# Product 3 of a unit placed behind product 1 of the next, and weight conversions held behind the gates, in a three-layer float32 kernel

## The chip, the cores and the metric

The kernel runs on one core of one Trainium2 chip. The metric is device time in microseconds (us). Engines are named as in the profile: PE is TensorE (PEld its weight loads), DVE is VectorE, ACT is ScalarE, POOL is GpSimd, and SP issues DMAs.

## The reference

Three layers in a row, all in float32:

```python
xread = softmax(x @ state.T / 8) @ state          # attention both ways, 8 batches x 8 heads
sread = softmax(state @ x.T / 8) @ x
x = concat(xread, sread)                          # 8 x 544 = 4352 tokens x 512
h = maximum(x[mask_e] @ w1[e], 0); x[mask_e] = h @ w2[e]     # 8 experts, 544 tokens each
g, val = x @ w_gate, x @ w_val                    # 512 -> 1536
out = (silu(g) * val) @ w_out                     # 1536 -> 512
```

The change touches only the third layer's first half, the gated products `x @ w_gate` and `x @ w_val`.

## The kernel before

**Stages.** Attention and routing run up to about 222 us, the experts' products up to 630 us, the gated passes from 630 to 1160 us, and the output products from 1160 to the end. Every float32 product is made of three matmuls on values split into a high and a low part.

**The gated passes.** A unit computes gate and value of 512 tokens for 256 of the 1536 hidden columns. There are two passes (`p`), each over nine groups of tokens (`groups`, lines 1159 and 1161: the experts 0 to 7, and the group E of the 256 tokens left over), each group with three units (`jj`), so 54 units. They are called unit 0 to unit 53 here; the code's `V = 27 * p + 3 * n + jj` (line 1249) is that number. The group E is the fifth of a pass, units 12 to 14 and 39 to 41.

A full unit (`unit`, from line 1116) multiplies blocks in the Winograd form of Strassen's method: seven block products in the order `PORDER = (1, 6, 7, 5, 2, 4, 3)` (line 868). Each product is a `hid`, 12 matmuls of 128x128 by 256 columns, so a full unit has 84; a unit of group E has four (48 matmuls). The passes have 4320 matmuls, all on line 1106.

The results go through four PSUM banks, each with two buffers, used by every second unit. Bank 1 takes product 1 and then, added to it, product 2; bank 2 takes product 6 and, after that has been read, product 4; bank 3 takes product 7; bank 4 takes product 5 and then, added to it, product 3. Behind the products stand, in this order: ACT's copy s1 of product 1 (line 1136), and on DVE u2 = product 6 + s1 (1139), u3 = product 7 + u2 (1142), `cs[:, :, 2]` = bank 4 + u3 (1145, the read of product 5), the gate of bank 1 (1148), `cs[:, :, 1]` = u3 - product 4 (1151), `cs[:, :, 0]` = bank 4 + u2 (1154, with product 3), and the gate of the three parts of cs (1155). A gate (`gate`, line 1112) is a silu on ACT (1113) and a multiplication on DVE (1114), 256 wide for bank 1 and 768 wide for cs. The unit's result m is then stored by SP (1157). s1, u2, u3 and cs have one buffer each, m has two.

**What runs beside it.** `after` (line 1226) splits the sums for the next group's operands into high and low parts between the products: one cast on ACT (871) and one subtraction on DVE (872) each. POOL makes the sums (897 to 900, 909 to 912), which SP stores (885) and loads again (890) in the second pass. SP also loads the inputs of the sums (926, 962, 1195).

The third layer's weights arrive as 64-bit numbers. `convert` (line 174) turns a block of 512 KB into float32: one instruction on ACT (179), three on DVE (181, 182, 184) and a store by SP (185); `load64` (line 162) loads a block (171). The first 16 conversions run beside the experts, the last 20 in the gated passes: conversion 16 + i is written behind the unit `CT[i]`, that is behind units 2, 4, ..., 22 and 30, 32, ..., 46, and the load of the next block behind it, the first ones behind units 0 and 28 (lines 1250 to 1255). The raw buffer is single in this stage.

**What sets the order.** The order in which instructions are written is a priority only. A planner goes through them with its own estimate of times and lists, for each engine, what is ready first, so that work can stand earlier in an engine's queue than it is written. Each engine, and SP's DMA queue, then runs its list in order. `tc.issue_after(ins)` holds the instructions written inside it behind `ins` in the list of `ins`'s engine. `hooks` is the kernel's dictionary of such instructions.

Of the kernel before, what the change touches and what calls it, by code (L numbers as in the profile page):

```python
# [26 lines left out]
AF = mybir.ActivationFunctionType  # L27
OP = mybir.AluOpType
# [3 lines left out]
B, H, S, D, NS = 8, 8, 512, 64, 32  # L32
# [25 lines left out]
def moe_kernel(ctx: ExitStack, tc: tile.TileContext, x, state, moe_w_gate, moe_w1, moe_w2,  # L58
               moe2_w_gate, moe2_w_val, moe2_w_out, out):
    nc = tc.nc  # L60
# [34 lines left out]
    xcs, hooks = {}, {}  # L95
# [1013 lines left out]
    def hid(p, a, b, start, stop):  # L1109
        product(p, [(lambda x, q, k=k: a[:, x, q, k], lambda y, k=k: b[:, y, k]) for k in range(2)], start, stop)  # L1110

    def gate(m, g, v):
        nc.scalar.activation(m, g, AF.Silu)  # L1113
        nc.vector.tensor_tensor(m, v, m, OP.mult)

    def unit(key, j, gi, after):
        m = cw.tile([128, 4, 256], F32, name="m", bufs=2)
        if gi == E:
            b1, b2 = bank(1), bank(2)
            hid(b1, WC[j, 1], Y[key, 1], True, False)  # L1120
            hid(b1, WC[j, 2], Y[key, 2], False, True)
            gate(m[:, 0], b1[:, 0], b1[:, 1])
            after(1)
            hid(b2, WC[j, 5], Y[key, 1], True, False)
            hid(b2, WC[j, 4], Y[key, 4], False, True)
            gate(m[:, 1], b2[:, 0], b2[:, 1])
            after(2)
            nc.sync.dma_start(m_d[gi][:, j], m[:, :2])
            return
        b1, b2, b3, b4 = (bank(i) for i in range(1, 5))  # L1130
        A = {n: WC[j, n] for n in PORDER}
        B = {n: Y[key, n] for n in PORDER}
        s1, u2, u3 = half("s1"), half("u2"), half("u3")
        cs = cw.tile([128, 2, 3, 256], F32, name="cs")
        hid(b1, A[1], B[1], True, False)
        nc.scalar.copy(s1, b1)
        after(1)
        hid(b2, A[6], B[6], True, True)
        nc.vector.tensor_tensor(u2, b2, s1, OP.add)
        after(6)  # L1140
        hid(b3, A[7], B[7], True, True)
        nc.vector.tensor_tensor(u3, b3, u2, OP.add)
        after(7)
        hid(b4, A[5], B[5], True, False)
        nc.vector.tensor_tensor(cs[:, :, 2], b4, u3, OP.add)  # L1145
        after(5)
        hid(b1, A[2], B[2], False, True)
        gate(m[:, 0], b1[:, 0], b1[:, 1])
        after(2)
        hid(b2, A[4], B[4], True, True)  # L1150
        nc.vector.tensor_tensor(cs[:, :, 1], u3, b2, OP.subtract)
        after(4)
        hid(b4, A[3], B[3], False, True)
        nc.vector.tensor_tensor(cs[:, :, 0], b4, u2, OP.add)  # L1154
        gate(m[:, 1:], cs[:, 0], cs[:, 1])
        after(3)
        nc.sync.dma_start(m_d[gi][:, j], m)

    groups = [[0, 1, 2, 3, E, 4, 5, 6, 7], [7, 6, 5, 4, E, 3, 2, 1, 0]]
    CT = tuple(range(2, 24, 2)) + tuple(range(30, 48, 2))  # L1160
# [60 lines left out]
    for p, n, gi, jj in hidden_units:  # L1221
        nxt = groups[p][n + 1] if n < E else None
        if jj == (p == n == 0) and nxt is not None:
            ysrc = y_sums(nxt, y_load(nxt, cw), cw)

        def after(step):
            if nxt is None or (gi == E) != (step < 3 and gi == E):
                return
            if gi == E:
                todo = {(0, 1): (0, 1), (0, 2): (1, 2), (1, 1): (2, 3), (1, 2): (3, 4), (2, 1): (4, 5), (2, 2): (5, 7)}  # L1230
                a, b = todo[jj, step]
                todo = PORDER[a:b]
            else:
                todo = {(1, 1): (1,), (1, 7): (6,), (1, 5): (7,), (2, 1): (5,), (2, 6): (2,), (2, 2): (4,),
                        (2, 5): (3,)}.get((jj, step), ())
            for m in todo:
                if m in ysrc:
                    y_combo((p, nxt), m, ysrc)

        if n == E and p == 0 and jj == 0:  # L1240
            wraw = pair_load(3, cw)
        unit(key, 3 * p + jj, gi, after)
        a = {1: 0, 3: 1, 4: 2, 6: 3}.get(n) if p else None
        if a is not None:
            if jj == 1:
                early = acts_load(*outs[a])
            elif jj == 2:
                acts_sums(outs[a][0], early, f"a{a}")
        V = 27 * p + 3 * n + jj
        if V in CT:  # L1250
            convert(16 + CT.index(V), cw)
        if V in CT or V in (0, 28):
            c = sum(t <= V for t in CT)
            if c < len(CT) and V != 22:
                load64(16 + c, cw, nc.sync)
        k = {2: 0, 5: 1, 7: 2}.get(n) if p else {1: 0, 3: 1, 6: 2}.get(n)
        if k is not None and jj == 1:
            early2 = out_load(k) if p else pair_load(3 + k, cw)
        if k is not None and jj == 2:
            if p:  # L1260
                out_sums(k, early2)
            else:
                pair_sums(early2, cw, f"w{3 + k}")
        if n == E and p == 0:
            src = pair_sums(wraw, cw, f"w{3 + jj}")
            if jj < 2:
                wraw = pair_load(4 + jj, cw)
            for m in PORDER:
                pair_combo(3 + jj, m, src)
        if n == E and p == 1:  # L1270
            src = out_sums(jj, out_load(jj))
            for m in PORDER:
                out_combo(jj, m, src)
            if jj == 1:
                acts[0] = acts_sums(outs[0][0], acts_load(*outs[0]), "a0")
                acts_prep(0, slice(0, 7))
        if jj == 2 and nxt is not None:
            key = (p, nxt)
        elif jj == 2 and p == 0:
            key = (0, gi)  # L1280
# [15 lines left out]
    def out_product(p, gi, jj, n, w, start, stop):  # L1296
        a, b = AO[gi, jj, n], WO[jj, w]
        product(p, [(lambda x, q, r=r: a[:, x, r, 128 * q:128 * q + 128], lambda y, r=r: b[:, y, r])
                    for r in range(2)], start, stop)

    BANK = {1: 1, 6: 2, 7: 3, 5: 4, 2: 1, 4: 2, 3: 3}
    for s, (gi, jj) in enumerate(outs):
        first, last = jj == 0, jj == 2
        if s + 1 < len(outs):
            acts[s + 1] = acts_sums(outs[s + 1][0], acts_load(*outs[s + 1]), f"a{s + 1}" if s + 1 < EARLY else None)
        if gi == E:
            if first:
                bx, by = bank(1), bank(2)
                o = rows()
            out_product(bx, gi, jj, 1, 1, first, False)  # L1310
            acts_prep(s + 1, slice(0, 3))
            out_product(bx, gi, jj, 2, 2, False, last)
            acts_prep(s + 1, slice(3, 5))
            if last:
                nc.scalar.copy(o[:, :, :256], bx)
            out_product(by, gi, jj, 3, 3, first, False)
            acts_prep(s + 1, slice(5, 7))
            out_product(by, gi, jj, 7, 7, False, last)
            if last:
                nc.vector.tensor_copy(o[:, :, 256:], by)  # L1320
                for q in range(2):
                    scatter(gi, q, o[:, q])
            continue
        if first:
            P = {n: bank(BANK[n]) for n in PORDER}
            s1, u2, u3 = half("s1"), half("u2"), half("u3")
            w = cw.tile([128, 2, 3, 256], F32, name="cs")[:, :, 0]
            oa, ob = rows(), rows()
        for m, n in enumerate(PORDER):
            out_product(P[n], gi, jj, n, n, first, last)  # L1330
            acts_prep(s + 1, slice(m, m + 1))
            if not last:
                continue
            if n == 1:
                nc.scalar.copy(s1, P[1])
            elif n == 6:
                nc.vector.tensor_tensor(u2, P[6], s1, OP.add)
            elif n == 7:
                nc.vector.tensor_tensor(u3, P[7], u2, OP.add)
            elif n == 2:  # L1340
                nc.vector.tensor_tensor(oa[:, :, :256], P[2], s1, OP.add)
            elif n == 5:
                nc.vector.tensor_tensor(ob[:, :, 256:], P[5], u3, OP.add)
                nc.vector.tensor_tensor(w, P[5], u2, OP.add)
            elif n == 4:
                nc.vector.tensor_tensor(ob[:, :, :256], u3, P[4], OP.subtract)
                for q in range(2):
                    scatter(gi, 2 + q, ob[:, q])
            else:
                nc.vector.tensor_tensor(oa[:, :, 256:], P[3], w, OP.add)  # L1350
                for q in range(2):
                    scatter(gi, q, oa[:, q])
# [29 lines left out]
```

## Time and profile before

| | us |
|---|---|
| median of 3 runs | 1431.58 (1429.67 to 1432.13) |
| the profiled execution's own time | 1430.67 |
| its span, first to last instruction | 1428.6 |
| mean granted clock of PE | 0.979 |

The span is the time between the first and the last instruction that the profile has; the execution's own time is what the median is made of. Engines run side by side, so busy times don't add up, and an engine's idle time counts only where the end of the kernel hangs on it. In a timeline, equal instructions that follow each other are merged into one row, and the brackets at a row's end tell how long the engine was idle before it and which instruction's end it waited for. The granted clock is the share of TensorE's full clock that it was given: 1.00 is 2.4 GHz, and the other level is 1.2 GHz, so a mean between the two tells how the time was divided.

### The profile page before, as it was taken

Reading aid. Unit: us, or ns where it says so; the run is one execution under the profiler, and the core shown is the slowest. Engines: PE = TensorE matmul, PEld = TensorE weight load, DVE = VectorE, ACT = ScalarE, POOL = GpSimd, SP = SyncE. Lnnn points to the kernel's source line nnn. Section 1 sums busy time; section 2 is a strip of 40 time slices with the busy share of each in tenths; the row PEclk is TensorE's granted clock in tenths of the full one; section 3 lists DMA queues with packets and bytes.
Section 4 is the critical chain, followed back from the end, with each engine's and each line's share of the span. In section 5 each row is a group of like instructions: output and inputs, shape, how many; then the busy total and the mean of one; then the engine's idle time right before and its main releaser. Section 6 shows DMA issues by size and latency. Waiting matters only on the chain.

```text
span 1428.6 us, 28982 instructions
## 1 busy us (share of the span) xinstructions
PE 1358.8 (95%) x11448; PEld 1318.8 (92%) x11449; DVE 1065.7 (75%) x2067; ACT 571.6 (40%) x1124; POOL 445.3 (31%) x388
## 2 busy tenths in 40 slices
PE   6998489999999999999989999999999999999997
PEld 5876288999999999999989999999999999999996
DVE  5889778877987664649776766777666588998982
ACT  5885123333433343434333333433333364444440
POOL 5776201010201010425241300112211008778862
PEclk9999699999999999999999999999999999999998
DMA  7542325543554464356674644756766394344431
GB/s 134 130 117 94 114 69 192 197 147 117 169 169 135 143 217 129 128 178 230 233 254 150 218 166 146 264 181 248 248 250 219 114 313 137 132 145 151 149 104 45
DMA packets 123335, 238.36 MB, mean 167 GB/s; under 512 B 47808, under 2 KB 57024, under 8 KB 116800
## 3 DMA queue, kind: packets, MB, share of 16 engines
q1 hardware_dynamic: 110096, 209.75, 44.0%
q0 software_dynamic: 5536, 17.83, 3.7%
q10 hardware_dynamic: 7568, 8.95, 2.1%
q8 instruction: 89, 1.46, 0.4%
q14 instruction: 46, 0.38, 0.1%
HBM read 153.65 MB, written 82.84 MB: 166 GB/s over the span
## 4 chain that ended last, share of the span: by engine, by line
PE 79%; DVE 8%; issue 5%; DMA 3%; ACT 3%; POOL 1%; SPq 0%; ACTq 0%; POOLq 0%; DVEq 0%
PE b L1106 48%; PE h L828 13%; PE y L847 4%; PE y L843 4%; PE y L844 4%; PE bt L807 1%; DVE yb L872 1%; DMA raw<-in_moe_w_val_dram 1%; DMA raw<-y_d 1%; PE pt L236 1%; PE ps L363 1%; PE acc L483 1%; ACT xu L325 1%; DMA xg<-xm_d,idx 0%; ACT RBh L220 0%
## 5 line engine op out<-in xcount | busy, mean ns | idle before, releaser
L1106 PE MATMUL b<-yb,w 128*128 128x256 f32 x4320 | 519.7, 283 | 10.0 <-DVE cs L1145 8.1
L1106 PEld LDWEIGHTS b<-yb,w 128*128 128x128 f32 x4320 | 517.2, 191 | 12.5 <-DVE cs L1145 9.2
L1106 PE MATMUL b<-w,yb 128*128 128x256 f32 x2160 | 257.5, 282 | 0.0
L1106 PEld LDWEIGHTS b<-w,yb 128*128 128x128 f32 x2160 | 257.4, 189 | 0.0
L828 PE MATMUL h<-xh,w 128*128 128x288 f32 (+1 forms) x1024 | 210.7, 298 | 1.5 <-issue 0.9
L828 PEld LDWEIGHTS h<-xh,w 128*128 128x128 f32 x1024 | 163.7, 191 | 3.2 <-DVE hl L833 1.1
L872 DVE TENSOR_TENSOR yb<-tt,yb 128x512 fp32r<-128x512 f32 x164 | 145.3, 897 | 16.8 <-ACT yb L871 14.3
L798 POOL DMA_INDIRECT xg<-xm_d,idx x38 | 44.2, 1163 | 361.3 <-PE bt L807 158.6
L897 POOL TENSOR_TENSOR tt<-raw 128x512 f32<-128x512 f32 (+1 forms) x33 | 42.8, 1299 | 340.8 <-DMA raw<-m_d 141.1
L828 PE MATMUL h<-xl,w 128*128 128x288 f32 (+1 forms) x512 | 148.2, 292 | 0.7 <-DVE xl L813 0.7
L872 DVE TENSOR_TENSOR yb<-raw,yb 128x512 fp32r<-128x512 f32 x127 | 131.6, 1043 | 15.9 <-ACT yb L871 12.0
L871 ACT CAST yb<-tt 128x512 fp32r<-128x512 f32 x164 | 100.6, 620 | 99.0 <-PE b L1106 81.4
L843 PE MATMUL y<-hh,w 128*128 128x288 f32 (+1 forms) x512 | 135.6, 291 | 2.3 <-ACT hh L832 2.3
L844 PE MATMUL y<-hh,w 128*128 128x288 f32 (+1 forms) x512 | 135.3, 290 | 0.0
L832 ACT ACTIVATE hh<-h 128x288 fp32r<-128x288 f32 (+1 forms) x128 | 50.7, 397 | 191.2 <-PE h L828 162.3
L833 DVE SCALAR_TENSOR_TENSOR hl<-h,hh 128x288 fp32r<-128x288 f32 (+1 forms) x128 | 55.9, 437 | 65.3 <-ACT hh L832 63.0
L871 ACT CAST yb<-raw 128x512 fp32r<-128x512 f32 x127 | 78.1, 620 | 59.9 <-PE b L1106 47.5
L843 PEld LDWEIGHTS y<-hh,w 128*128 128x128 f32 x512 | 96.5, 188 | 2.5 <-ACT hh L832 2.5
L828 PEld LDWEIGHTS h<-xl,w 128*128 128x128 f32 x512 | 97.1, 191 | 1.7 <-DVE xl L813 0.9
L844 PEld LDWEIGHTS y<-hh,w 128*128 128x128 f32 x512 | 96.6, 189 | 0.0
L847 PE MATMUL y<-hl,w 128*128 128x288 f32 (+1 forms) x512 | 89.2, 292 | 0.0
L1113 ACT ACTIVATE m<-cs 128x768 f32<-128x768 f32 x48 | 40.6, 846 | 100.5 <-DVE cs L1154 99.8
(261 smaller groups left out, 2039.4 us busy)
## 6 DMA issues: line engine op xcount, KB each, us to landing
raw<-in_moe_w_dram SPq DMA_DIRECT2D x64, 512.0 KB
raw<-m_d SPq DMA_DIRECT2D x28, 1024.0 KB
m_d<-m SPq DMA_DIRECT2D x48, 512.0 KB
raw<-v_d SPq DMA_DIRECT2D x32, 512.0 KB
raw<-y_d SPq DMA_DIRECT2D x14, 1024.0 KB
xm_d<-xm SPq DMA_DIRECT2D x8, 1024.0 KB
y_d<-ys SPq DMA_DIRECT2D x16, 512.0 KB
sums_dy<-tt SPq DMA_DIRECT2D x32, 256.0 KB
```

The source lines that it names most:

```text
L798: hooks["g"] = nc.gpsimd.indirect_dma_start(out=xg[:n], out_offset=None, in_=xm_d, in_offset=bass.IndirectOffsetOnAxis(ap=idx[i][:n, j:j + ...
L828: hooks["p"] = nc.tensor.matmul(ph, W[i][0][k][q == 1][:, fs], (xl if q == 2 else xh)[:, k, :T], start=(n == 0), stop=(n == 11)).ins
L832: relu[16 * i + 8 * hf + f] = hooks["hh"] = nc.scalar.activation(hh, ph, AF.Relu).ins
L833: hooks["h"] = nc.vector.scalar_tensor_tensor(hl, ph, 0.0, f32(hh), op0=OP.max, op1=OP.subtract).ins
L843: nc.tensor.matmul(p[d], wh[:, f % 2, ds_], hh, start=(f == 0), stop=False)
L844: nc.tensor.matmul(p[d], wl[:, f % 2, ds_], hh, start=False, stop=False)
L847: nc.tensor.matmul(p[d], wh[:, f % 2, ds_], hl, start=False, stop=(f == 7))
L871: nc.scalar.copy(hi, src)
L872: nc.vector.tensor_tensor(lo, src, f32(hi), OP.subtract)
L897: nc.gpsimd.tensor_tensor(S1, a21, a22, OP.add)
L1106: nc.tensor.matmul(p[:, q], a(x, q), b(y), skip_group_check=True, start=start and not (q or n or m), stop=stop and q == 1 and n == last an ...
L1113: nc.scalar.activation(m, g, AF.Silu)
```

## The change

`unit` no longer runs product 3 with what hangs on it (the add to cs, the gate of cs, the store of m) at its end. It puts them into a function `third` on the list `late3`, and the next unit calls `finish` behind its own product 1 (behind its first half product in group E; the output stage calls it behind its products, which matters for the last unit only). The conversions and the loads of 64-bit blocks go on a second list, `later`. `finish` runs them behind `third`, and holds what they have on ACT behind the last silu written and what they have on DVE behind the last gate's multiplication, which are those of `third`, or, after a unit of group E, of that unit's second gate. No instruction is added or taken away.

```diff
--- before.py
+++ after.py
@@ -1110,14 +1110,24 @@
         product(p, [(lambda x, q, k=k: a[:, x, q, k], lambda y, k=k: b[:, y, k]) for k in range(2)], start, stop)
 
     def gate(m, g, v):
-        nc.scalar.activation(m, g, AF.Silu)
-        nc.vector.tensor_tensor(m, v, m, OP.mult)
+        hooks["silu"] = nc.scalar.activation(m, g, AF.Silu).ins
+        hooks["gate"] = nc.vector.tensor_tensor(m, v, m, OP.mult).ins
+
+    late3, later = [], []
+
+    def finish():
+        while late3:
+            late3.pop(0)()
+        while later:
+            with tc.issue_after(hooks["silu"]), tc.issue_after(hooks["gate"]):
+                later.pop(0)()
 
     def unit(key, j, gi, after):
         m = cw.tile([128, 4, 256], F32, name="m", bufs=2)
         if gi == E:
             b1, b2 = bank(1), bank(2)
             hid(b1, WC[j, 1], Y[key, 1], True, False)
+            finish()
             hid(b1, WC[j, 2], Y[key, 2], False, True)
             gate(m[:, 0], b1[:, 0], b1[:, 1])
             after(1)
@@ -1135,6 +1145,7 @@
         hid(b1, A[1], B[1], True, False)
         nc.scalar.copy(s1, b1)
         after(1)
+        finish()
         hid(b2, A[6], B[6], True, True)
         nc.vector.tensor_tensor(u2, b2, s1, OP.add)
         after(6)
@@ -1150,11 +1161,15 @@
         hid(b2, A[4], B[4], True, True)
         nc.vector.tensor_tensor(cs[:, :, 1], u3, b2, OP.subtract)
         after(4)
-        hid(b4, A[3], B[3], False, True)
-        nc.vector.tensor_tensor(cs[:, :, 0], b4, u2, OP.add)
-        gate(m[:, 1:], cs[:, 0], cs[:, 1])
         after(3)
-        nc.sync.dma_start(m_d[gi][:, j], m)
+
+        def third():
+            hid(b4, A[3], B[3], False, True)
+            nc.vector.tensor_tensor(cs[:, :, 0], b4, u2, OP.add)
+            gate(m[:, 1:], cs[:, 0], cs[:, 1])
+            nc.sync.dma_start(m_d[gi][:, j], m)
+
+        late3.append(third)
 
     groups = [[0, 1, 2, 3, E, 4, 5, 6, 7], [7, 6, 5, 4, E, 3, 2, 1, 0]]
     CT = tuple(range(2, 24, 2)) + tuple(range(30, 48, 2))
@@ -1248,11 +1263,11 @@
                 acts_sums(outs[a][0], early, f"a{a}")
         V = 27 * p + 3 * n + jj
         if V in CT:
-            convert(16 + CT.index(V), cw)
+            later.append(lambda V=V: convert(16 + CT.index(V), cw))
         if V in CT or V in (0, 28):
             c = sum(t <= V for t in CT)
             if c < len(CT) and V != 22:
-                load64(16 + c, cw, nc.sync)
+                later.append(lambda c=c: load64(16 + c, cw, nc.sync))
         k = {2: 0, 5: 1, 7: 2}.get(n) if p else {1: 0, 3: 1, 6: 2}.get(n)
         if k is not None and jj == 1:
             early2 = out_load(k) if p else pair_load(3 + k, cw)
@@ -1328,6 +1343,7 @@
             oa, ob = rows(), rows()
         for m, n in enumerate(PORDER):
             out_product(P[n], gi, jj, n, n, first, last)
+            finish()
             acts_prep(s + 1, slice(m, m + 1))
             if not last:
                 continue
```

## Rows read from the trace of the kernel before

**Rows 1.** The page, part 1: busy us (share) xinstructions by engine.

```profile
PE 1358.8 (95%) x11448; PEld 1318.8 (92%) x11449; DVE 1065.7 (75%) x2067; ACT 571.6 (40%) x1124; POOL 445.3 (31%) x388
```

**Rows 2.** Windows: us, busy us (instructions) by engine, PEclk, DMA share, GB/s.

```profile
650.00:670.00 20.00, 17.22 (x131) 16.80 (x130) 19.86 (x27) 10.45 (x19) 9.03 (x6) 0.91 0.68 234
...
730.00:750.00 20.00, 15.51 (x116) 15.14 (x116) 14.54 (x19) 4.35 (x7) 5.62 (x5) 0.91 0.76 265
750.00:820.00 70.00, 70.00 (x591) 70.00 (x590) 49.22 (x71) 22.83 (x41) 17.77 (x12) 1.00 0.52 180
...
1160.00:1410.00 250.00, 250.00 (x2101) 250.00 (x2100) 212.25 (x233) 111.00 (x182) 173.52 (x118) 1.00 0.42 147
```

**Rows 3.** Timeline of PE, 630 to 830: start, us, line, [idle before <- releaser].

```profile
630.82 26.85 PE L1106 MATMUL b<-yb,w 128*128 128x256 f32 x228
658.42 1.67 PE L1106 MATMUL b<-yb,w 128*128 128x256 f32 x12 [0.75 <-DVE u L1139]
662.12 32.20 PE L1106 MATMUL b<-yb,w 128*128 128x256 f32 x252 [2.03 <-DVE cs L1145]
695.57 7.36 PE L1106 MATMUL b<-yb,w 128*128 128x256 f32 x60 [1.25 <-DVE cs L1145]
703.69 33.59 PE L1106 MATMUL b<-yb,w 128*128 128x256 f32 x276 [0.76 <-ACT s L1136]
741.77 87.36 PE L1106 MATMUL b<-yb,w 128*128 128x256 f32 x720 [4.49 <-DVE cs L1145]
```

**Rows 4.** Timeline of PE, 805 to 1420: two last waits, output stage.

```profile
829.58 269.06 PE L1106 MATMUL b<-yb,w 128*128 128x256 f32 x2256 [0.46 <-DVE u L1139]
1098.91 61.62 PE L1106 MATMUL b<-yb,w 128*128 128x256 f32 x516 [0.28 <-DVE cs L1145]
...
1160.37 257.54 PE L1106 MATMUL b<-w,yb 128*128 128x256 f32 x2160
```

**Rows 5.** Timeline of DVE, 735 to 743: the longest wait of PE.

```profile
738.51 0.94 DVE L181 TENSOR_SCALAR tt<-raw 128x512 int32<-128x512 int32 x1 [2.30 <-DMA raw<-in_moe_w_val_dram]
739.55 1.56 DVE L182 SCALAR_TENSOR_TENSOR tt<-tt 128x512 int32<-128x512 int32 x1
741.04 0.68 DVE L1145 TENSOR_TENSOR cs<-b,u 128x512 f32<-128x512 f32 x1
```

**Rows 6.** Timeline of SP, 728 to 745: the load that this conversion reads.

```profile
732.54 0.43 SPq L171 DMA_DIRECT2D raw<-in_moe_w_val_dram  x1
```

**Rows 7.** Timeline of DVE, 682 to 695: a conversion ahead of product 3's add.

```profile
685.32 1.49 DVE L184 SCALAR_TENSOR_TENSOR tt<-raw,tt 128x512 int32<-128x512 int32 x1
686.73 0.68 DVE L1154 TENSOR_TENSOR cs<-b,u 128x512 f32<-128x512 f32 x1
```

**Rows 8.** Timeline of ACT, 690 to 700: a conversion that waits for its load.

```profile
696.71 0.67 ACT L179 ACTIVATE tt<-raw 128x512 f32<-128x512 f32 x1 [5.99 <-DMA raw<-in_moe_w_val_dram]
```

**Rows 9.** L181 and L1114, 630 to 770: ns min/median/max, first and last start.

```profile
L181 DVE TENSOR_SCALAR tt<-raw x8: 414/424/1512, 661.1 to 760.5; 128x512 int32<-128x512 int32 x8
...
L1114 DVE TENSOR_TENSOR m<-cs,m x12: 942/959/2046, 645.2 to 769.0; 128x768 f32<-128x768 f32 x12
```

**Rows 10.** Timeline of DVE, 750 to 758: product 3's add and gate.

```profile
754.88 0.69 DVE L1154 TENSOR_TENSOR cs<-b,u 128x512 f32<-128x512 f32 x1 [0.75 <-PE b L1106]
756.49 0.96 DVE L1114 TENSOR_TENSOR m<-cs,m 128x768 f32<-128x768 f32 x1 [0.91 <-ACT m L1113]
```

**Rows 11.** Waits of SP, 630 to 1160: us in total, times, longest.

```profile
SPq L1157 <- DVE m L1114: 132.0, 40, 9.8
```

**Rows 12.** L184 and L872, 630 to 1180: count, ns min/median/max, first and last start.

```profile
L184 DVE SCALAR_TENSOR_TENSOR tt<-raw,tt x20: 676/692/1810, 664.0 to 1043.7; 128x512 int32<-128x512 int32 x20
...
L872 DVE TENSOR_TENSOR yb<-raw,yb x58: 678/687/1784, 648.2 to 1179.8; 128x512 fp32r<-128x512 f32 x58
```

**Rows 13.** Timelines of DVE and POOL, 654 to 662: gate beside sum.

```profile
655.72 2.04 DVE L1114 TENSOR_TENSOR m<-cs,m 128x768 f32<-128x768 f32 x1
...
655.27 1.68 POOL L909 TENSOR_TENSOR tt<-raw 128x512 f32<-128x512 f32 x1 [2.75 <-DVE yb L872]
```

## The prediction

> **What bounds the kernel now.** I read the engines' busy shares first: PE is busy 95% of the span and VectorE (DVE) 75% [rows 1]. On the whole, then, there is little to win; the question is where PE's other 5% lie in the gated passes, the only stage that the change touches. The windows come next [rows 2]: 750 to 820 us and the output stage hold no idle time on PE, while 650 to 670 and 730 to 750 fall short, and their mean granted clock is 0.91 where the others have 1.00. The timeline of PE then names every gap [rows 3, 4]. There are seven: 0.75 and 2.03 us near 660 (stall A), 1.25 at 695 (B), 0.76 at 703 (C), 4.49 at 741 (D), 0.46 at 829 (E), 0.28 at 1098 (F), 10.0 us in all.
>
> The pace without gaps comes from the output stage, whose matmuls have the same size: 257.54 us for 2160 is 119.2 ns for one [rows 4], so 1.43 us for a product of 12 and 10.0 us for a unit of 84. The passes have 4320 matmuls, which at that pace need 515.1 us; they run from 630.82 to 1160.37 [rows 3, 4], 529.5 us. **The room is 14.5 us**: the 10.0 us of gaps, and 4.5 us that run slowly behind them. The 252 matmuls after A took 32.20 us for 30.0, the 720 after D 87.36 for 85.8, the 276 after C 33.59 for 32.9, the 60 after B 7.36 for 7.15 [rows 3]. The lower clock of the two windows, time at 1.2 of 2.4 GHz, is in these excesses. So A costs 5.0 us, B 1.45, C 1.45, D 6.0, E and F 0.75.
>
> What ends the gaps is not PE's own input. Four of the seven end on L1145, the read of product 5 from bank 4, into which product 3 accumulates: two products, 2.9 us, lie between product 5 and product 3, and DVE was later than that. For D the timeline of DVE shows why [rows 5]: a conversion's L181 sat 2.30 us in front of L1145 until its load landed at 738.5, L182 followed, and L1145 ran at 741.04. That load was only issued at 732.54 [rows 6]. For B, a conversion's L184 of 1.49 us ran ahead of product 3's add, at 686.73 [rows 7], and everything behind it on DVE moved. For C, ScalarE (ACT) stood 5.99 us before a conversion's L179 until the load landed at 696.71 [rows 8], and the splits and the gate queued behind. A has only a small part from a conversion (an L181 of 0.42 us at 661.1, shortly before the read of product 5 [rows 9]); there DVE is full, 19.86 of 20 us [rows 2].
>
> The conversions run far ahead of the text: by 760.5 eight are done, while the twelfth 768-wide gate (unit 11) starts at 769.0 [rows 9]; the text puts the eighth behind unit 16.
>
> **The change, part by part.**
>
> *Conversions behind a gate.* No instruction is added: 20 conversions keep one ACT and three DVE instructions, one store and one load each. What moves is their place: conversion k now runs in unit 3, 5, 7 and so on, behind the silu and the multiplication of the unit before, two units (20 us) apart. The eighth conversion goes from unit 11 to unit 17; up to 760 us, where A to D lie, there are five (units 3 to 11) instead of eight. The raw buffer is single, so a load follows the previous conversion; it then leads the next by nearly 20 us, where D's took 5.97 us from issue (732.54) to use (738.51) [rows 5, 6]. So D, B and C lose their cause: 6.0 + 1.45 + 1.45 = 8.9 us.
>
> What a held conversion costs at its new place isn't in the trace. From below: conversions eight to twenty, from 760.5 on [rows 9], stood beside gaps of 0.46 and 0.28 us only, so nothing. From above: as much as they cost so far, 8.9 us, the stalls only re-placed. A gain beyond the lost stalls is excluded, since the work is the same. I take 2 us, near the lower end, because thirteen of the twenty are of that kind.
>
> *Product 3 behind the next product 1.* The matmuls stay 4320. Slack between product 5 and product 3 grows from two products to three, by 1.43 us. Of A's 2.03 us that leaves 2.03 - 1.43 - 0.42 = 0.18. A's 0.75 stays: product 4 is the 20th product of PE either way (unit 0 runs six, then one slides in front), and it waits for u2's read, behind the gate on DVE. With a gap of 0.9 instead of 2.78 us, most of the 2.2 us of slow matmuls behind it should go too; I keep 0.5. So A gives 3.5 of its 5.0. F (0.28) goes, E (0.46, on u2) stays.
>
> *The tail of product 3.* Add to end of gate takes 757.45 - 754.88 = 2.57 us [rows 10], now 1.43 us later against the next unit. The single buffers cs and u2 tie it to the next unit: cs is written again after product 5, three products (4.3 us) behind product 3, before it was four. 4.3 - 2.57 leaves 1.7 us in an undisturbed unit, and a lag there is DVE's alone until product 3 of the next unit is due, three products later. Cost nothing; the cover is that slack.
>
> *The store of m and SP's queue.* SP already waits 132.0 us for the gates, 40 times, up to 9.8 us [rows 11]. Each store moves back by 1.43 us, and with it the loads, sums and conversion stores queued behind. They feed work at least a unit ahead; at E and F, where splits wait for loads, it may add up to 1.4 us each. From below zero; both ends lie inside the 2 us and its upper end. The last unit's product 3 falls behind the first output product: 12 matmuls change place, nothing else.
>
> **Sum.** 8.9 + 3.5 + 0.3 - 2.0 = 10.7 us off the profiled execution's 1430.67 us, 1420.0. Its span is 1428.6, so 2.1 us lie around it and stay. The median of the runs, 1431.58, is 0.9 above this execution: **1420.9 us**. The floor, all of the room, is 1431.6 - 14.5 = 1417.1.
>
> **A rule weighed.** The rows show DVE's instructions with two operands from SBUF at 0.69 us in the median and 1.81 at most, the splits at 0.69 and 1.78 [rows 12]; the 768-wide gate, 0.96 otherwise, took 2.04 beside a sum on POOL [rows 13]. By the medians a conversion is 0.42 + 0.69 + 0.69 = 1.8 us of DVE; at the slowest 1.51 [rows 9] + 1.56 [rows 5] + 1.81 = 4.9 (L182's median taken like L184's). The Trainium skill, "SBUF — State Buffer", Who interferes with whom, says that a DVE instruction with two SBUF inputs contends with a GpSimd instruction that reads SBUF, and that the later one waits in full. The rows agree that it happens; by the medians it is the exception. A change that only moves conversions can move them into POOL's sums: that is the second rival.
>
> **The rivals.** What this measurement can tell from no change is about 0.2%, 2.9 us.
>
> First, *the slack helps, the holding doesn't*: conversions stall the queues again at their new places, as often as before. Then the gain is the slack alone, min(gap, 1.43) at the four L1145 waits: 1.43 + 1.25 + 1.43 + 0.28 = 4.4, so 1427.2. For it: the ACT and DVE queues are in order, and a held conversion can still wait for its load. Against: the load's lead of nearly two units.
>
> Second, *contention*: four held conversions in the busy first 100 us meet POOL's sums in all three instructions, 3.1 us more each, 12.4 us on a full DVE. 12.7 - 12.4 is next to no change: 1431.3. For it: POOL works 9 of the 20 us in 650 to 670 [rows 2]. Against: the medians.
>
> Third, *the changed order isn't taken up on PE*: the planner lists product 3 before the next product 1 all the same. Then the conversions alone count: 8.9 + 0.4 of A - 2 = 7.3, so 1424.3.
>
> Fourth, *slower*: the loads of held conversions come late, since SP's queue stands at the stores [rows 11], and each such conversion blocks DVE as D did, for 6.0 us. From three such blocks on it outweighs everything: 18 - 12.7 = 5.3, so 1436.9. For it: a load sits behind up to 9.8 us of SP wait. Against: 9.8 + 6.0 is still under 20.
>
> **How the numbers follow.** Forecast 0.67, first rival 0.13, second 0.08, third 0.05, fourth 0.07. Faster by over 0.2%: 0.67 + 0.13 + 0.05 = 0.85; within 0.2%: 0.08; slower: 0.07. The range reaches from the floor, a microsecond lower for the spread of the runs, to the first rival with a microsecond on top: 1416 to 1428; the second and fourth, 0.15, lie outside.
>
> **What would show it.** PE's gaps at 695, 703 and 741 gone; the L181 rows 20 us apart and the last near 1085 instead of 1041; L1145's waits on PE at most 0.3 us; the passes at 519 us or so. It is wrong if the L181 rows still carry waits for loads that PE's gaps answer to, if DVE is full beyond 700 us, or if new gaps in the passes add up to over 5 us.

## The result and the profile after

The changed kernel took 1418.4 us (median of 4 runs, 1415.97 to 1420.64), the kernel before 1431.5 us beside it: a ratio of 0.9911, interval 0.9894 to 0.9929. The profiled execution took 1420.64 us, 10.0 less than that of before. The forecast, 1420.9 us and a range of 1416 to 1428, holds.

The page's first part and the windows answer to [rows 1] and [rows 2]:

```profile
PE 1357.2 (96%) x11449; PEld 1318.0 (93%) x11449; DVE 1053.9 (74%) x2067; ACT 571.7 (40%) x1124; POOL 441.8 (31%) x388
```

```profile
650.00:670.00 20.00, 17.54 (x136) 17.33 (x135) 19.72 (x28) 10.55 (x19) 10.93 (x7) 0.91 0.65 240
...
730.00:750.00 20.00, 20.00 (x169) 20.00 (x168) 11.18 (x19) 4.72 (x8) 5.66 (x4) 1.00 0.34 117
```

DVE's work is what it was within 12 us, and PE's share rose by one point. The window from 730 to 750, which had 15.51 of 20 us busy and a clock of 0.91, is full at 1.00; the one from 650 to 670 is not.

The timeline of PE answers to [rows 3] and [rows 4]:

```profile
630.62 19.77 PE L1106 MATMUL b<-yb,w 128*128 128x256 f32 x168
652.85 125.82 PE L1106 MATMUL b<-yb,w 128*128 128x256 f32 x1044 [2.46 <-DVE cs L1156]
779.58 50.62 PE L1106 MATMUL b<-yb,w 128*128 128x256 f32 x423 [0.91 <-DVE u L1150]
...
1148.52 1.60 PE L1106 MATMUL b<-w,yb 128*128 128x256 f32 x12
1149.96 1.60 PE L1106 MATMUL b<-yb,w 128*128 128x256 f32 x12
1151.40 256.10 PE L1106 MATMUL b<-w,yb 128*128 128x256 f32 x2148
```

B, C and D are gone: 1044 matmuls follow each other from 652.85 on. Of A's two gaps one is left, 2.46 us at 652, still on the read of product 5, which is L1156 in the new kernel (L1145 before). A gap of 0.91 us at 779 is new. The last product 3 stands between output products, as the three last rows show. The passes' 4320 matmuls and 12 of the output stage run from 630.62 to 1151.40; without the 12 that is 519.3 us, where it was 529.5.

The conversions, on the line L181 in the passes (count, ns min/median/max, first and last start), answer to [rows 9]:

```profile
L181 DVE TENSOR_SCALAR tt<-raw x20: 408/419/1514, 670.6 to 1084.5; 128x512 int32<-128x512 int32 x20
```

The last one starts at 1084.5 instead of 1041.9 us.

### The profile page after: what moved, and what is told of

It reads as the page before. It is cut to its first block, busy times and chain, and to the rows that moved or that the text cites. A ratio compares the mean times of both kernels' runs of the same rounds, so it can differ in the third digit from the quotient of the medians.

```text
span 1418.1 us, 28991 instructions
## 1 busy us (share of the span) xinstructions
PE 1357.2 (96%) x11449; PEld 1318.0 (93%) x11449; DVE 1053.9 (74%) x2067; ACT 571.7 (40%) x1124; POOL 441.8 (31%) x388
## 4 chain that ended last, share of the span: by engine, by line
PE 81%; DVE 6%; issue 5%; ACT 3%; DMA 2%; POOL 1%; ACTq 0%; POOLq 0%; SPq 0%; DVEq 0%
PE b L1106 50%; PE h L828 13%; PE y L847 4%; PE y L843 4%; PE y L844 4%; PE bt L807 1%; PE pt L236 1%; PE ps L363 1%; PE acc L483 1%; ACT xu L325 1%; ACT RBh L220 1%; DVE yb L872 1%; DMA xg<-xm_d,idx 1%; DMA raw<-y_d 0%; ACT zb L288 0%
## 5 line engine op out<-in xcount | busy, mean ns | idle before, releaser
L872 DVE TENSOR_TENSOR yb<-tt,yb 128x512 fp32r<-128x512 f32 x164 | 144.9, 897 | 21.7 <-ACT yb L871 20.9
L872 DVE TENSOR_TENSOR yb<-raw,yb 128x512 fp32r<-128x512 f32 x127 | 129.8, 1030 | 38.7 <-ACT yb L871 38.4
L847 PEld LDWEIGHTS y<-hl,w 128*128 128x128 f32 x512 | 74.1, 191 | 0.0
```

The lines of the kernel that those rows point to most:

```text
L847: nc.tensor.matmul(p[d], wh[:, f % 2, ds_], hl, start=False, stop=(f == 7))
L872: nc.vector.tensor_tensor(lo, src, f32(hi), OP.subtract)
```

## The experiments

The runs came in three groups, each with the kernel before beside it on the same chip; its medians there were 1434.8 us for the first four runs, 1432.8 for the next four and 1434.5 for the last two, which ran on another chip than the first eight. So ratios are compared, not times. Gaps are those of PE in the passes, from the profiled execution. The diffs are against the changed kernel. All compute the whole result.

### Each part alone

**Slack alone.**

```diff
-            later.append(lambda V=V: convert(16 + CT.index(V), cw))
+            convert(16 + CT.index(V), cw)
-                later.append(lambda c=c: load64(16 + c, cw, nc.sync))
+                load64(16 + c, cw, nc.sync)
```

> Product 3 moved behind the next product 1; conversions and their loads written and listed as before. Holding theory (the prediction's sum): the slack alone gives min(gap, 1.43) at the reads of product 5, 4.4 us, so about 1427, with D still a gap of some 3 us near 740 and a conversion's wait for its load in front of it. Rival (the slack does it all, the holding adds nothing): 1418, no gap near 740.

Measured: 1434.72 us, ratio 0.9994 (0.9982 to 1.0006). Nothing is gained, less than either theory said. The timeline of PE, the larger gaps:

```profile
654.41 37.66 PE L1106 MATMUL b<-yb,w 128*128 128x256 f32 x312 [2.16 <-DVE cs L1156]
...
697.08 5.93 PE L1106 MATMUL b<-yb,w 128*128 128x256 f32 x48 [1.63 <-DVE cs L1156]
...
707.38 31.60 PE L1106 MATMUL b<-yb,w 128*128 128x256 f32 x252 [2.40 <-DVE u L1150]
740.20 3.14 PE L1106 MATMUL b<-yb,w 128*128 128x256 f32 x24 [1.23 <-DVE u L1150]
747.82 86.41 PE L1106 MATMUL b<-yb,w 128*128 128x256 f32 x708 [4.48 <-DVE cs L1156]
836.20 324.01 PE L1106 MATMUL b<-yb,w 128*128 128x256 f32 x2710 [1.96 <-DVE u L1150]
```

and the timeline of DVE at the longest:

```profile
746.23 0.94 DVE L181 TENSOR_SCALAR tt<-raw 128x512 int32<-128x512 int32 x1 [4.62 <-DMA raw<-in_moe_w_val_dram]
747.09 0.68 DVE L1156 TENSOR_TENSOR cs<-b,u 128x512 f32<-128x512 f32 x1
```

D is there as before: L181 waits 4.62 us for its load, and the read of product 5 stands right behind it. With it, 2.16 and 1.63 us still end on that read, 8.3 us in all, where the kernel before had 8.1: a product more of slack has not made these gaps smaller in sum. Others are added. They end on L1150, the read of product 6 by u2, which product 4 waits for when it writes bank 2 again. The distance from product 5 to product 3 grew to three products, but the one from product 6 to product 4 was three and stayed three. Before, u2's gaps were 0.75 and 0.46 us [rows 3, 4]; here they are 2.40, 1.23, 1.96 and a small one of 0.27. The profiled execution, 1437.66 us, is one of the longest of its twelve, so its gaps are rather larger than usual.

**Holding alone.**

```diff
-        late3.append(third)
+        third()
```

> Conversions held behind the gates, product 3 at its unit's end as before. Holding theory: B, C and D are gone (8.9 us) and 0.4 of A, less up to 2 us at the new places: 1422 to 1424, gaps of PE only near 660 and small ones. Rival (the slack does it all): 1431, the gaps of before in other places.

Measured: 1422.5 us, ratio 0.9912 (0.9897 to 0.9927), as much as the whole change. The timeline of PE:

```profile
650.99 11.39 PE L1106 MATMUL b<-yb,w 128*128 128x256 f32 x82 [2.00 <-DVE cs L1156]
662.73 384.99 PE L1106 MATMUL b<-yb,w 128*128 128x256 f32 x3228 [0.36 <-DVE cs L1156]
1048.93 10.18 PE L1106 MATMUL b<-yb,w 128*128 128x256 f32 x84 [1.21 <-DVE cs L1156]
```

Between 662.73 and 1047.7 no gap stands on PE. The passes took 521.1 us here; in two profiles of the changed kernel they took 519.3 and 520.9. So the gain comes from what the change does to the conversions; product 3's new place adds nothing to it that these intervals can tell.

### Where the holding works

**Written later, without the edges.**

```diff
         while later:
-            with tc.issue_after(hooks["silu"]), tc.issue_after(hooks["gate"]):
-                later.pop(0)()
+            later.pop(0)()
```

> Both parts, but conversions only written later, without the edges that hold them. Holding theory: the planner lists them early again, so this behaves like the slack alone, about 1427, with gaps that end on a conversion's wait for its load. Rival (the place in the text is enough): 1418, conversions 20 us apart.

Measured: 1423.62 us, ratio 0.992 (0.9905 to 0.9934). The timeline of PE, in which u2's line is L1149 (this kernel has a line less), and what ACT's part of the conversions, L179, waited for (us, times):

```profile
702.71 31.41 PE L1106 MATMUL b<-yb,w 128*128 128x256 f32 x252 [1.89 <-DVE u L1149]
735.49 415.62 PE L1106 MATMUL b<-yb,w 128*128 128x256 f32 x3492 [1.37 <-DVE u L1149]
```

```profile
  DMA raw<-in_moe_w_val_dram: 12.8, 3
  DMA raw<-in_moe_w_out_dram: 8.8, 4
  DMA raw<-in_moe_w_gate_dram: 5.9, 2
```

The planner did list the conversions early again: the first six run in the same units as before. They wait for their loads, 27.5 us on ACT and 6.8 us on DVE. Yet most of the gain is there, 0.0080 of 0.0089, so my theory's expectation of 1427 us missed: the edges (the two `issue_after` holds) are not shown to add anything, and a wait for a load does not by itself cost PE anything. Why writing them later is enough was not taken apart. One difference stands in the rows: with slack alone, and in the kernel before, DVE waited 4.62 and 2.30 us directly ahead of the read of product 5, and there the longest gaps are; here none of its four waits stands there. This run has product 3 at its new place too; written later with product 3 at its old place was not tried.

**The first four held.**

```diff
-            later.append(lambda V=V: convert(16 + CT.index(V), cw))
+            later.append(lambda V=V: convert(16 + CT.index(V), cw)) if V < 9 else convert(16 + CT.index(V), cw)
...
-                later.append(lambda c=c: load64(16 + c, cw, nc.sync))
+                later.append(lambda c=c: load64(16 + c, cw, nc.sync)) if V < 9 else load64(16 + c, cw, nc.sync)
```

> Both parts, but only the conversions behind units 2, 4, 6 and 8 are written later and held; the other sixteen as before. If only the conversions of the crowded first 100 us cost anything: 1418 to 1420, as with all held. If every conversion listed early costs (rival: each freely listed one stalls its queue now and then): a gap or two between 740 and 1050, 1423 or more.

Measured: 1433.99 us, ratio 0.9988 (0.9977 to 1.0). The timeline of PE:

```profile
653.82 99.04 PE L1106 MATMUL b<-yb,w 128*128 128x256 f32 x816 [2.47 <-DVE cs L1156]
...
786.44 40.33 PE L1106 MATMUL b<-yb,w 128*128 128x256 f32 x324 [2.59 <-DVE u L1150]
829.15 1.66 PE L1106 MATMUL b<-yb,w 128*128 128x256 f32 x12 [2.38 <-ACT s L1146]
834.97 104.40 PE L1106 MATMUL b<-yb,w 128*128 128x256 f32 x864 [4.16 <-DVE u L1150]
```

and two rows of ACT's:

```profile
793.13 0.67 ACT L179 ACTIVATE tt<-raw 128x512 f32<-128x512 f32 x1 [7.80 <-DMA raw<-in_moe_w_out_dram]
...
827.72 0.62 ACT L871 CAST w<-raw 128x512 fp32r<-128x512 f32 x1 [13.66 <-DMA raw<-v_d]
```

The first 100 us are clean, 816 matmuls without a gap, as with all held. But the next conversions, left free, then come one behind the other, each as soon as its load is listed as done, and one of them holds ACT for 7.80 us at 793. At 827 ACT stands 13.66 us before a split of the next pass's weights, whose inputs are loaded late, and copies and casts queue behind: the gaps of 2.38 and 4.16 us come behind this split, not behind a conversion. So it isn't that only the first 100 us are crowded: with those held, the gaps came later. The profiled execution, 1438.6 us, is the longest of its twelve.

**Late loads, early places, and both.** Two things change for a held conversion: its load has a lead of about a unit and a half, and it runs later. The next three set out to take them apart. The first issues each load only behind the store of the unit's result, ahead of its own conversion:

```diff
+            later.append(lambda V=V: load64(16 + CT.index(V), cw, nc.sync))
             later.append(lambda V=V: convert(16 + CT.index(V), cw))
-        if V in CT or V in (0, 28):
-            c = sum(t <= V for t in CT)
-            if c < len(CT) and V != 22:
-                later.append(lambda c=c: load64(16 + c, cw, nc.sync))
...
+            with tc.issue_after(hooks["silu"]), tc.issue_after(hooks["gate"]), tc.issue_after(hooks["store"]):
```

> The changed kernel, but each block's load is issued only behind the store of the unit's result, right ahead of its own conversion, so that every conversion runs shortly behind its load as in the kernel before, at the places of the changed one. If the holding pays because it gives the loads a lead (theory now): the conversions wait for their loads on ACT and DVE again and PE has gaps behind some of them; at least the 8.9 us of B, C and D come back, 0.997 or more, at most 20 x 6.0 us on top. If it pays because the conversions' work leaves the crowded units (rival): the places are unchanged, so 0.991.

The second keeps the lead and holds the first eleven conversions in the units in which the kernel before had them, or next to them:

```diff
-    CT = tuple(range(2, 24, 2)) + tuple(range(30, 48, 2))
+    CT = (1, 2, 3, 4, 5, 7, 8, 10, 11, 13, 14) + tuple(range(30, 48, 2))
...
-            if c < len(CT) and V != 22:
+            if c < len(CT) and V != 14:
```

> The changed kernel, but the first eleven conversions held behind the gates of units 1, 2, 3, 4, 5, 7, 8, 10, 11, 13 and 14, so that they run in the units in which the kernel before had them, each with its load a unit or more ahead. If the crowding of the early units is the larger cause (theory now, after the late loads gave back only 0.0026): gaps of PE between 660 and 790 return, 0.995 or more. If the lead of the loads is the larger cause (rival): 0.991 to 0.992, no gaps there beyond those of the changed kernel.

The third does both:

> As the run with the early places, and each load issued only right ahead of its conversion as well. If crowding and late loads add up: the gain is gone, 0.998 to 1.002. If only one of them counts: as the one with that cause alone.

The changed kernel itself ran beside the first of them.

> The changed kernel itself, beside the three that follow: 0.991 of the time before, as measured.

| | loads with a lead | late loads |
|---|---|---|
| late places | 0.9913 (0.9896 to 0.9931) | 0.9939 (0.9922 to 0.9957) |
| early places | 0.9935 (0.9921 to 0.9950) | 0.9984 (0.9967 to 1.0000) |

Late loads alone give back 0.0026 and early places alone 0.0022 of a gain of 0.0087, each with an interval that still overlaps that of the changed kernel; both together give back 0.0071, some four fifths, and that is clear of the other three. The parts are not quite single: a late load also moves its conversion some 5 us on in its unit, from behind the gate's multiplication to behind product 4's read (the first L181 from 670.6 to 675.2 us). The timelines of PE say more than the sums. Late loads at the late places:

```profile
652.92 124.40 PE L1106 MATMUL b<-yb,w 128*128 128x256 f32 x1032 [2.47 <-DVE cs L1156]
779.96 2.50 PE L1106 MATMUL b<-yb,w 128*128 128x256 f32 x12 [2.64 <-ACT s L1146]
```

Every conversion waits, 61.6 us in all on ACT (us, times):

```profile
  DMA raw<-in_moe_w_out_dram: 38.4, 12
  DMA raw<-in_moe_w_val_dram: 12.0, 4
  DMA raw<-in_moe_w_gate_dram: 11.2, 4
```

and still there is no gap from 652.92 to 777. The one at 779 is 2.64 us, where the changed kernel has 0.91: DVE waited 1.40 us for a load at 771 and then ran three splits in 4.67 us. Early places, loads with a lead:

```profile
652.32 125.69 PE L1106 MATMUL b<-yb,w 128*128 128x256 f32 x1044 [2.46 <-DVE cs L1156]
...
822.55 230.09 PE L1106 MATMUL b<-yb,w 128*128 128x256 f32 x1920 [4.29 <-ACT s L1146]
```

Again there is no gap from 652.32 to 778. What this kernel loses is mainly one gap, 4.29 us at 822, and there ACT waits for something else:

```profile
818.90 0.62 ACT L871 CAST w<-raw 128x512 fp32r<-128x512 f32 x1 [13.35 <-DMA raw<-v_d]
```

That is the early split of the next pass's weights again. With the conversions done early, the planner loads these weights early and lists the split where its load has not landed. In the changed kernel the same split comes some 16 us later and leaves no gap.

Both together:

```profile
706.51 75.72 PE L1106 MATMUL b<-yb,w 128*128 128x256 f32 x624 [2.79 <-DVE cs L1156]
785.38 14.44 PE L1106 MATMUL b<-yb,w 128*128 128x256 f32 x108 [3.16 <-DVE u L1150]
```

Now the stretch of B, C and D has gaps again, 0.34 and 0.57 us at 679 and 690 and 2.79 at 706, and 3.16 us follow at 785. The timelines of DVE show what makes the difference, first this kernel's ahead of the gap at 706, then that of the late places with late loads, at a wait that leaves no gap:

```profile
697.01 0.43 DVE L181 TENSOR_SCALAR tt<-raw 128x512 int32<-128x512 int32 x1 [3.23 <-DMA raw<-in_moe_w_val_dram]
...
700.65 1.82 DVE L1114 TENSOR_TENSOR m<-cs,m 128x768 f32<-128x768 f32 x1
...
702.99 2.86 DVE L872 TENSOR_TENSOR yb<-tt,yb 128x512 fp32r<-128x512 f32 x2
705.77 0.68 DVE L1156 TENSOR_TENSOR cs<-b,u 128x512 f32<-128x512 f32 x1
```

```profile
715.93 0.43 DVE L181 TENSOR_SCALAR tt<-raw 128x512 int32<-128x512 int32 x1 [2.05 <-DMA raw<-in_moe_w_val_dram]
...
720.16 0.96 DVE L1114 TENSOR_TENSOR m<-cs,m 128x768 f32<-128x768 f32 x1
```

In both, L181 waits for its load, 3.23 and 2.05 us. At the early place the gate's multiplication and the splits come behind it, beside POOL's sums: 1.82 us for the gate and 2.86 for two splits, and L1156 is late for product 3. These sums waited themselves: a conversion's two tiles come from the same six buffers, `tt`, as POOL's sums, and POOL stood idle for 7.85 us before the first of them, until this conversion's L182 was done. At the late place the gate takes 0.96 and nothing has piled up. The gap of 3.16 us is of this kind too, with three splits of 4.71 us in all behind waits of 0.98 and 1.27 us.

D is of another kind, for no split stands near it [rows 5]. The kernel before has a wait of nearly the same length that left no gap, 30 us ahead of D:

```profile
708.70 0.43 DVE L181 TENSOR_SCALAR tt<-raw 128x512 int32<-128x512 int32 x1 [2.15 <-DMA raw<-in_moe_w_gate_dram]
...
710.08 0.42 DVE L1114 TENSOR_TENSOR m<-b,m 128x256 f32<-128x256 f32 x1
```

That one stood behind the read of product 5, ahead of the gate of bank 1; PE ran on from 703.69 to 737.28 [rows 3]. D's 2.30 us stood directly ahead of the read of product 5 and went with 4.49 us. So a wait's length alone does not tell its price. In the rows shown, long gaps go with waits directly ahead of the read of product 5, or ahead of a run of splits. That is read from single stretches; no run moved one wait and left all else in place.

### What is left of A

**Splits held.** The splits of the second group of tokens are held on DVE behind the read of product 5 in unit 1.

```diff
-        nc.vector.tensor_tensor(cs[:, :, 2], b4, u3, OP.add)
+        hooks["cs2"] = nc.vector.tensor_tensor(cs[:, :, 2], b4, u3, OP.add).ins
...
+                if p == n == 0:
+                    todo = {(1, 5): (1, 6, 7), (2, 1): (5,), (2, 6): (2,), (2, 2): (4,), (2, 5): (3,)}.get((jj, step), ())
...
-                if m in ysrc:
+                if m in ysrc and p == n == 0:
+                    with tc.issue_after(hooks["cs2"]):
+                        y_combo((p, nxt), m, ysrc)
+                elif m in ysrc:
                     y_combo((p, nxt), m, ysrc)
```

> The changed kernel with the splits of the second group of tokens held on DVE behind the read of product 5 in unit 1. If the gap that is left near 652 (2.46 us) comes from two splits of 1.77 and 1.16 us and their place ahead of that read: the gap shrinks to under 0.5 and some 3 us go with the slow matmuls behind it, 0.989. Rival (DVE is full there whatever the order): the gap only moves on by some products, 0.991.

In the changed kernel, DVE's timeline ahead of the gap at 652 was this:

```profile
646.77 1.77 DVE L872 TENSOR_TENSOR yb<-raw,yb 128x512 fp32r<-128x512 f32 x1
648.47 2.05 DVE L1114 TENSOR_TENSOR m<-cs,m 128x768 f32<-128x768 f32 x1
...
651.04 1.16 DVE L872 TENSOR_TENSOR yb<-tt,yb 128x512 fp32r<-128x512 f32 x1
652.12 0.68 DVE L1156 TENSOR_TENSOR cs<-b,u 128x512 f32<-128x512 f32 x1
```

The splits and the gate took 1.77, 1.16 and 2.05 us, and L1156 came last. Measured with the splits held: 1418.8 us, ratio 0.9903 (0.9886 to 0.9919), against 1421.12 and 0.9913 for the changed kernel beside it. The gaps of PE:

```profile
650.35 7.34 PE L1106 MATMUL b<-yb,w 128*128 128x256 f32 x60 [1.61 <-DVE cs L1156]
657.97 13.14 PE L1106 MATMUL b<-yb,w 128*128 128x256 f32 x108 [0.28 <-DVE u L1150]
672.19 104.39 PE L1106 MATMUL b<-yb,w 128*128 128x256 f32 x876 [1.07 <-DVE cs L1156]
777.52 269.99 PE L1106 MATMUL b<-yb,w 128*128 128x256 f32 x2268 [0.94 <-DVE u L1150]
```

The gap shrank to 1.61, not under 0.5. DVE shows what stood in the way then:

```profile
649.28 0.42 DVE L1114 TENSOR_TENSOR m<-b,m 128x256 f32<-128x256 f32 x1 [2.12 <-ACT m L1113]
649.62 0.68 DVE L1156 TENSOR_TENSOR cs<-b,u 128x512 f32<-128x512 f32 x1
```

The planner had moved the gate of bank 1 ahead of L1156, and that multiplication waited 2.12 us for its silu. Two small gaps, 0.28 and 1.07, came in later, so that the three make 2.96 us where one of 2.46 was: the rival, that the gap only moves on, fits these rows better. The times, 1418.23 to 1419.12 against 1418.95 to 1421.48 for the changed kernel beside it, point to some 2 us, but the intervals of the ratios overlap, and the passes took 519.3 us, as in the changed kernel's first profile; they only began 1.7 us earlier. So no worth of this hold is shown.

**The same, product 3 at its unit's end.**

```diff
-        late3.append(third)
+        third()
```

> The same hold of the splits, with product 3 at its unit's end and the conversions held. If the later product 3 adds nothing beside the holding: as the run with the splits held in the changed kernel, within 0.001. If the later product 3 covers what the splits leave: 0.001 to 0.003 slower than that.

Measured: 1422.9 us, ratio 0.9924 (0.9906 to 0.9943), 0.0021 above the run before it. PE's gaps in the first units are 1.32 and 1.82 us here. It points to a small worth of product 3's place once the conversions are held, but the intervals overlap, and without the splits' hold no such worth was seen; what it is worth stays open within 0.002.

## Why the prediction was right, and where its steps were off

**The room and the gaps: right.** The passes were to take some 519 us and took 519.3, B, C and D were to go and went, the conversions were to end near 1085 us and end at 1084.5. The size, 10.7 us, agrees with the 10.0 between the two profiled executions and, within the interval of the ratio, with the 13.1 between the medians; the changed kernel's profiled execution was the slowest of its four. That the sum came out is in part luck: 3.8 us of it (3.5 of A and 0.3 of F) were to come from product 3's place, which shows no worth beside the holding, and the conversions brought more than their 6.9 us (8.4 by the passes' time, 529.5 before and 521.1 with the holding alone).

**The cause of B, C and D: in part.** I put D down to a conversion that waits for a late load directly ahead of the read of product 5, and the rows still say so: the same wait and the same gap, 4.62 and 4.48 us, come back with slack alone. But late loads are not the whole cause. The late-load run waits at nearly every conversion, though not at that point, and has no gap in that stretch; and written later without the edges, the conversions still run early and wait, and most of the gain is there. The step "D, B and C lose their cause" gave the right 8.9 us, since the holding takes away the waits and changes the places at once; which of the two each gap needed was not taken apart for B and C.

**The slack: wrong.** The first rival priced it at 4.4 us alone, as min(gap, 1.43) at each read of product 5. Alone it gave nothing. The step took each gap as one semaphore's business. With the slack, the gaps on product 5's read were 8.3 us, not 8.1 less 4.4, and bank 2, whose slack the change leaves at three products, stopped PE for 5.9 us where it had been 1.2.

**A: wrong.** I expected gaps of 0.9 us together and 3.5 us saved. The read of product 5 was to stop PE for at most 0.3 us. There is one gap of 2.46 on it, with 1044 matmuls behind it in 125.82 us for 124.5, so A costs 3.8 us and saved 1.2. It is the same mistake: product 3 was let later by 1.43 us, but L1156 came later as well, behind splits and a gate of 1.77, 2.05 and 1.16 us.

**The cost of the held conversions: about right.** 2 us were set aside. The new gap at 779 is 0.91 us, and in the second profile of the changed kernel there are gaps of 1.49, 0.31 and 0.72 at 780, 1050 and 1061. L179 waited for loads 0.8 us in all in that second profile, too little to make these gaps; what makes them was not taken apart.

**The rivals.** The changed order was taken up on PE, so the third rival did not come about; its price for the conversions alone, 7.3 us, was too low, for they alone gave 0.0088 of the time, some 12.6 us. Contention, the second, is in the rows: the gate took 2.05 us beside a sum at A, and 1.82 at the gap with early places. It was too weak to take the gain. I called it the exception by the medians, and the rows say when it comes: of the 20 L184 of the kernel before, seven took 1.17 to 1.81 us, and each of the seven ran while a sum ran on POOL; the other 13 took 0.68 or 0.69, and none of them did. For this the Trainium skill, "SBUF — State Buffer", Who interferes with whom, states a mechanism (a DVE instruction with two SBUF inputs contends with a GpSimd instruction that reads SBUF). The rows agree with it as far as they go; no run here takes the sums away. The fourth rival priced a late load at 6.0 us for each conversion; the late-load run made all 20 late for 3.7 us in all.

**Left open.** Why the slack covers nothing where conversions are free was not taken apart: a second buffer for product 4, which would give bank 2 the same slack, was not tried. Nor was a second raw buffer, which would give loads a lead at the old places without any hold, nor tiles of their own for the conversions.

## What to carry to other kernels

When an engine's list is made by a planner, look at what it listed early and what that work waits for: the conversion at D ran at 738.5 us, 38 us ahead of where the changed kernel has it, and its wait there went with the longest gap of the critical engine. Writing such work later, or tying it to a point at which it is harmless, brought nearly the whole gain here, with no work taken away; holding only its first fifth brought next to nothing. Slack given at one dependency brought nothing here while the engine behind it stayed late, so look at the other dependencies on that engine before pricing it.

## What the runs showed of the hardware

Twenty conversions that waited for their loads, 61.6 us on ACT and 23.3 on DVE, cost only 0.0026 of the time, some 3.7 us, while a single wait of 2.30 us on DVE directly ahead of the read of product 5 had gone with a gap of 4.49 us on PE. I had not expected the price of a wait to differ that much with what stands behind it.

In the passes of the kernel before, no L184, and no 768-wide gate or split that stands alone in its row, ran longer than usual without a sum on POOL beside it: seven, six and fourteen were longer, and all of them had one.
